# Sparse attention and a gated FFN on one core: two dense groups of 128 tokens become one of 256, and the instruction order is a new one

## The chip, the cores and the metric

The kernel runs on one core of a Trainium2 chip. Times are device microseconds from launch to end; the time of a kernel is the median of its runs. A profiled execution gives one trace, whose times count from the span's start. PE is the matrix engine (TensorE), DVE the vector engine, ACT the scalar engine, POOL is GpSimd, and SP (SyncE) issues DMAs, as POOL does. PE writes into PSUM, eight banks of 2 KB per partition, from which ACT and DVE read.

## The reference

Block-sparse attention over 4 batches, 8 heads, 768 positions and 64 dims, followed by a gated feed-forward over all 3072 tokens:

```python
scores = scale * np.matmul(q, k.transpose(0, 1, 3, 2))
mask = np.abs(blk_i - blk_j) <= 1            # blocks of 32: own and neighbours
mask = mask | (blk_i == 0) | (blk_j == 0) | (blk_i == 23) | (blk_j == 23)
for qb in range(24):
    for kb in sampled_blocks[qb]:            # three sampled blocks per query block
        mask[qb*32:(qb+1)*32, kb*32:(kb+1)*32] = True
attn = softmax(np.where(mask, scores, -1e9))
attn_out = np.matmul(attn, v)                # -> x: 3072 tokens x 512
gate = 1.0 / (1.0 + np.exp(-(x @ w_gate)))   # 512 x 1536
out = (gate * (x @ w_val)) @ w_out           # 1536 x 512
```

## The kernel before, in words

**Attention.** Each batch has 24 query blocks. Blocks 0 and 23 see all keys and are done "edge-wise" (`dsc`, `dmx`, `dex`, `dsl`, `dtp`, `dte`, `dpv`, `dxe`). The other 22 are done as eleven pairs, or steps: (4,5), (6,7) ... (18,19), (2,3), (20,21), (1,22). A name like `sc0_18` is an operation, batch 0, and the first block of its pair. A step is, in turn: `kw` copies the neighbour keys and `kg` (POOL, line 712) the three sampled key blocks into a key tile KG; `sc` makes scores and mask on PE (lines 784 and 773) in two PSUM banks; `mx` (DVE, line 796) takes the row maximum; two `ex` (ACT, line 806, two exponentials each) make P and free one bank each; `rz` inverts the sums; two `sl` scale P, on ACT (line 828), DVE (830, two instructions) or POOL (824, one instruction of 512 columns); `tp` transposes P on PE (842); `te` copies that to PTS on DVE or ACT (848); `pv` multiplies with V on PE (860); `xe` copies the result into XT, the input of the dense stage. V is stored to a scratch in DRAM (`scr`), from which windows of neighbours (`w`) and sampled blocks (`vg`) are read into the tiles V1 and V2, A to D; the two edge blocks of V are copied into these by `vfl`, on POOL two copies (line 641).

**Dense stage.** Tokens go through in groups of 128-token tiles; `groups` in TUNE lists the (batch, tile) pairs of each. For each of 12 chunks of 128 hidden units, `pg` and `pu` (line 1029, four matmuls each: one slot) multiply the group's columns of XT with `w_gate` and `w_val`, into one PSUM bank each; `th` (ACT, line 1038) takes tanh of the first and frees its bank, `h` (DVE, line 1043) multiplies it with the second and frees that. Then `py` (line 1060) makes 128 rows of the output, `ys` evicts them and `st` stores them. A group needs its tiles' attention: tile (0, 1) is blocks 4 to 7 of batch 0, tile (0, 2) blocks 8 to 11. All groups use banks 5, 6 and 7, but the first `two` groups use only 5 and 6:

```python
def pg_of(g):
    return bk(5, 6) if g < TUNE["two"] else pgb if g < len(GROUPS) - 2 else pgb + bk(4, 3, 2, 1, 0)
```

**Order.** The program order on every engine is written out in the string ORDER, one item per operation: `sl0_40:A` says that this operation runs on ACT; digits behind the engine choose among buffers or banks; `+14` behind a PE operation puts 14 fillers ahead of it, matmuls of a zero tile WZ into bank 7 whose result nobody reads (line 1083). Every engine does its items in that order and waits for what an item needs. POOL's list holds its DMAs as well: the loads of q, k and v, of the weights (`wg0`, `wv0` ... `wo2`, in thirds) and some windows.

Of the kernel before, what the change touches and what calls it, by code (L numbers as in the profile page):

```python
# [55 lines left out]
wg1:G sc0_4:P3+14 mx0_4:D6 kw0_10:G0 sc0_6:P1+1 kg0_10:G dsl0_00:D ex0_40:A0 mx0_6:D0 dtp0_00:P00+5 ex0_41:A w0_4:G0
vg0_5:S dte0_00:D regPOOL0_1:G ex0_60:A2 dtp0_01:P0+4 vg0_7:S rz0_4:D sl0_41:D ex0_61:A sc0_8:P0 sc0_10:P3 kw0_14:D2
sl0_40:A rz0_6:D mx0_8:D7 vg0_4:S kw0_12:A1 tp0_4:P11+3 dte0_01:A mx0_10:D1 kg0_12:G vg0_6:S sl0_60:A dpv0_0:P0+4
w0_8:G0 sl0_61:D ex0_80:A1 te0_4:D wv1:G vg0_8:S ex0_81:A sc0_12:P2+2 tp0_6:P10 kw0_18:G1 ex0_100:A0 vg0_11:S
kg0_14:G te0_6:D ex0_101:A mx0_12:D0 pv0_4:P1+3 wg2:G vg0_9:S kg0_18:G rz0_8:D rz0_10:D ex0_120:A2 xe0_4:D dxe0_0:D  # L60
vg0_10:S sl0_100:A sl0_80:G pv0_6:P0+8 sl0_101:A sc0_14:P0 wv2:G xe0_6:D kw0_2:A2 sl0_81:D w0_12:G0 pg0_0:P00+2
pu0_0:P1 th0_0:A0 tp0_10:P12 h0_0:D kw0_16:D0 pg0_1:P10 regSP0_1:S mx0_14:D1 pu0_1:P0 kg0_16:G th0_1:A2 tp0_8:P00
ex0_121:A pg0_2:P10 h0_1:D wo0:G te0_10:D pu0_2:P0+1 th0_2:A2 ex0_140:A0 pg0_3:P10 vg0_13:S h0_2:D regPOOL0_2:G
rz0_12:D sl0_120:D pu0_3:P0 th0_3:A0 sl0_121:A pg0_4:P10+1 h0_3:D te0_8:D pu0_4:P0 th0_4:A2 vg0_12:S ex0_141:A
sc0_16:P2 h0_4:D pg0_5:P10 mx0_16:D5 pv0_8:P1 kw0_20:A0 pu0_5:P0 w0_16:S0 tp0_12:P00 th0_5:A1 kg0_20:G ex0_160:A1
h0_5:D vg0_15:S rz0_14:D sl0_141:D pg0_6:P00+1 pu0_6:P1 te0_12:D th0_6:A0 w0_2:G0 xe0_8:A sc0_18:P0 h0_6:D pg0_7:P00
mx0_18:D4 pu0_7:P1 ex0_161:A pv0_10:P0 vg0_14:S wo1:G th0_7:A1 ex0_180:A2 h0_7:D pg0_8:P00+2 rz0_16:D xe0_10:D
kg0_2:G th0_8:A2 vg0_19:S sl0_160:D pu0_8:P0+3 pg0_9:P10 kw0_1:G1 sl0_161:D sc0_2:P2 h0_8:D th0_9:A1 ex0_181:A wo2:G
pu0_9:P0 mx0_2:D7 vg0_18:S pg0_10:P10 tp0_16:P02 kg0_1:G th0_10:A0 pu0_10:P1 h0_9:D ex0_20:A1 pg0_11:P00 h0_10:D
sl0_140:G vg0_16:S pu0_11:P1 th0_11:A1 ex0_21:A sc0_20:P0+1 h0_11:D vfl0A:G pg1_0:P10 mx0_20:D3 pu1_0:P0 th1_0:A0  # L70
pg1_1:P20 pu1_1:P1 th1_1:A2 tp0_14:P11 te0_16:A h1_0:D h1_1:D pg1_2:P00 rz0_18:D sl0_181:D pu1_2:P1 ldv10:G0
vg0_17:S pg1_3:P20 th1_2:A2 rz0_2:D pv0_12:P0 h1_2:D th1_3:A0 sl0_20:G pu1_3:P2 xe0_12:A pg1_4:P10 h1_3:D te0_14:D
regSP0_2:S pu1_4:P2 w0_1:G0 th1_4:A0 ex0_200:A0 pg1_5:P10 h1_4:D sl0_180:D pu1_5:P0 pg1_6:P20 sl0_21:D th1_5:A2
pv0_14:P0 th1_6:A0 h1_5:D ldk10:G1 pu1_6:P2 vg0_3:S xe0_14:A pg1_7:P10 h1_6:D pu1_7:P0 ldq10:G2 pg1_8:P20 th1_7:A2
sc0_1:P2 h1_7:D th1_8:A0 vfl0B:G ex0_201:A pu1_8:P1 vg0_21:S mx0_1:D2 pg1_9:P00 tp0_18:P10 th1_9:A2 pu1_9:P2
pg1_10:P00 h1_8:D rz0_20:D tp0_2:P01 h1_9:D vg0_20:S th1_10:A0 sl0_201:D ex0_10:A2 pu1_10:P2 pg1_11:P10 h1_10:D
pu1_11:P2 th1_11:A0 sl0_200:A dsc0_23:P02 h1_11:D ex0_11:A py1_0:P2 dmx0_231:D1 vg0_2:S rz0_1:D dmx0_230:D4
dex0_231:A0 dex0_230:A1 dsl0_231:D py0_0:P1 sl0_11:D te0_2:A ys1_0:D0 dsl0_230:D te0_18:A vsh1:D3 dtp0_230:P00
ys0_0:A1 rrk1:G0 scr1:S dtp0_231:P1 dte0_230:D dte0_231:D pv0_16:P0 tp0_20:P12 xe0_16:D te0_20:D rrq1:G1 trk100:P0
evk100:D trk102:P1 st0_0:S pv0_18:P0 evk102:D st1_0:S dpv0_23:P1 regPOOL1_2:G vg0_1:S xe0_18:D pg2_0:P10 dxe0_23:D  # L80
pu2_0:P0 vg0_22:S th2_0:A0 trq102:P0 pg2_1:P10 evq102:D trk101:P1 th2_1:A2 h2_0:D trk103:P0 gv1:S evk101:A pu2_1:P2
ldv20:G0 evk103:D pg2_2:P00 h2_1:D kw1_1:A0 pu2_2:P1 kfl11:G trq101:P1 kfl10:G th2_2:A1 trq100:P0 evq101:D kg1_1:G
pg2_3:P20 evq100:A h2_2:D trq103:P1 pu2_3:P1 kw1_2:A1 evq103:D th2_3:A1 sc1_1:P1 kg1_2:G pv0_2:P1 mx1_1:D3 pg2_4:P00
ldk20:G1 pu2_4:P2 th2_4:A2 xe0_2:D ex1_10:A0 kw1_20:G0 pg2_5:P00 sl0_10:D pv0_20:P0 ex1_11:A h2_3:D sc1_2:P0 vfl1C:S
h2_4:D tp0_1:P12 mx1_2:D4 kw1_4:G1 th2_5:A0 pu2_5:P1 kg1_20:G te0_1:A w1_2:S0 pg2_6:P00 h2_5:D pu2_6:P2 th2_6:A2
rz1_1:D regPOOL1_0:G sl1_11:D pg2_7:P10 regSP1_2:S h2_6:D pu2_7:P0 th2_7:A0 xe0_20:D pg2_8:P20 ex1_20:A1 pu2_8:P1
sl1_10:D pv0_1:P1 h2_7:D th2_8:A2 kg1_4:G ex1_21:A pg2_9:P20 h2_8:D w1_1:S0 sc1_20:P2 vfl1D:G th2_9:A2 pu2_9:P0
mx1_20:D1 xe0_1:A vg1_3:S pg2_10:P10 pu2_10:P2 th2_10:A0 h2_9:D tp1_1:P00 ex1_200:A2 h2_10:D pg2_11:P10 vg1_21:S
kw1_6:D0 pu2_11:P0 rz1_2:D th2_11:A0 sl1_21:G pg3_0:P20 h2_11:D sc1_4:P0 th3_0:A1 vg1_22:S sl1_20:G ex1_201:A
py2_0:P0 mx1_4:D6 kg1_6:G rrk2:D2 vg1_1:S ex1_40:A0 ex1_41:A vsh2:D1 pu3_0:P2 vg1_2:S tp1_2:P11 kw1_8:A1 te1_1:D  # L90
# [1025 lines left out]
```

## Time and profile before

| | us |
|---|---|
| three runs | 339.26, 339.18, 337.01 |
| median | 339.18 |
| profiled execution | 338.43 |
| its span, first to last instruction | 336.5 |
| busy: PE, DVE, ACT, POOL | 318.1, 230.8, 232.4, 128.1 |
| PE busy with fillers (102) | 28.5 |

An instruction row of the profile's order of time gives start, duration, engine, line, operation, output and inputs, shapes, a count where several were merged, and in brackets the idle time of the engine ahead of it with what ended it. A row of the table of stretches gives the stretch, its length, the busy time of PE, of PE's weight loads (PEld), DVE, ACT and POOL with their instruction counts, then the granted TensorE clock (1.00 is full), the DMA share and the GB/s. A row on a group gives count, busy time, mean ns of one, idle time ahead; a row on a tile or line gives shortest, median and longest ns, and first and last start. Matmuls are pipelined: the next can start before the one ahead has ended.

### The profile page before, as it was taken

The numbers are of one execution on the slowest core, as the hardware profiler recorded it, in microseconds if no ns is written. First come the engines' busy times: TensorE is split into PE (matmuls) and PEld (weight loads), VectorE is DVE, ScalarE is ACT, GpSimd is POOL, SyncE is SP. The second block draws the span as 40 slices with busy tenths as digits, with TensorE's granted clock in tenths as the row PEclk, the third lists the DMA queues.
The fourth block names the chain that finished last, engine by engine and source line by source line (L and its number), as shares of the span: only waits on it lengthen the run. The fifth ranks groups of instructions, "written<-read, shape, count | busy, mean of one in ns | idle before, by whom it ended". The sixth has DMA issues, their size and how long they took to land.

```text
span 336.5 us, 11685 instructions
## 1 busy us (share of the span) xinstructions
PE 318.1 (95%) x4230; PEld 194.5 (58%) x4230; DVE 230.8 (69%) x493; ACT 232.4 (69%) x663; POOL 128.1 (38%) x376
## 2 busy tenths in 40 slices
PE   8999887899999789999998999999999999999995
PEld 3545565748776667796555655555645555554442
DVE  3677787777888896697878687698986855423330
ACT  1759785782789887866886788898999764523320
POOL 6575774614777433353184414522522100000000
PEclk9999997999999999999999999999999999999999
DMA  7999999986976655476984344241242352011002
GB/s 115 206 233 216 179 260 209 181 155 186 150 168 100 162 171 157 133 116 129 216 162 125 92 123 134 69 132 33 51 130 70 108 150 52 7 57 64 0 31 94
DMA packets 42873, 43.14 MB, mean 128 GB/s; under 512 B 6560, under 2 KB 39200, under 8 KB 42720
## 3 DMA queue, kind: packets, MB, share of 16 engines
q0 software_dynamic: 14736, 15.93, 29.5%
q1 hardware_dynamic: 28080, 26.47, 27.0%
q8 instruction: 33, 0.54, 0.7%
q14 instruction: 24, 0.20, 0.2%
HBM read 47.10 MB, written 9.44 MB: 168 GB/s over the span
## 4 chain that ended last, share of the span: by engine, by line
PE 70%; DMA 8%; DVE 8%; ACT 7%; issue 3%; POOL 2%; SPq 1%; POOLq 0%; DVEq 0%; ACTq 0%
PE pall L1029 32%; PE pall L1060 17%; PE pall L860 6%; PE pall L842 4%; DMA stg<-in_v_dram 4%; ACT P L806 4%; PE pall L784 3%; PE pall L551 2%; PE pall L970 2%; DVE HT L1043 2%; DMA V2C<-scr 2%; DMA scr<-XL 2%; ACT TH L1038 2%; PE pall L950 1%; DVE NM L796 1%
## 5 line engine op out<-in xcount | busy, mean ns | idle before, releaser
L1038 ACT ACTIVATE TH<-pall 128x512 f32<-128x512 f32 (+2 forms) x108 | 49.1, 459 | 54.7 <-PE pall L1029 46.7
L806 ACT ACTIVATE P<-pall,NM 128x256 f16<-128x256 f32 x176 | 81.3, 477 | 6.5 <-DVE NM L796 5.7
L1043 DVE SCALAR_TENSOR_TENSOR HT<-TH,pall 128x512 f16<-128x512 f32 (+2 forms) x108 | 53.6, 506 | 33.3 <-PE pall L1029 27.3
L1060 PE MATMUL pall<-wo,HT 128*128 128x512 f16 x288 | 65.5, 379 | 0.2 <-DVE HT L1043 0.2
L796 DVE TENSOR_REDUCE NM<-pall 128x4 f32<-128x1024 f32 x44 | 53.6, 1220 | 14.5 <-PE pall L773 9.7
L712 POOL COPY KG<-KT 128x64 f32 x264 | 53.0, 251 | 24.8 <-PE pall L773 18.4
L1029 PE MATMUL pall<-XT,wv 128*128 128x256 f16 (+2 forms) x336 | 56.1, 290 | 4.4 <-DVE HT L1043 3.7
L1029 PE MATMUL pall<-XT,wg 128*128 128x256 f16 (+2 forms) x336 | 56.0, 290 | 3.7 <-DVE HT L1043 1.9
L1029 PEld LDWEIGHTS <-wg 128*128 128x128 f16 x432 | 37.8, 98 | 28.9 <-issue 8.2
L1029 PEld LDWEIGHTS <-wv 128*128 128x128 f16 x432 | 37.8, 99 | 26.7 <-issue 7.3
L1060 PEld LDWEIGHTS <-HT 128*128 128x128 f16 x288 | 26.9, 98 | 32.0 <-issue 1.2
L806 ACT ACTIVATION_READ_ACCUMULATOR P<-pall,NM 128x1 f32 x176 | 36.8, 209 | 0.0
L824 POOL TENSOR_TENSOR P<-P,ZZ 128x512 f16<-128x512 f16 x19 | 19.6, 1039 | 31.8 <-DVE ZZ L815 12.9
L1083 PE MATMUL pall<-WZ 128*128 128x512 f16 x102 | 28.5, 414 | 1.2 <-DVE WZ L371 1.2
L828 ACT ACTIVATE P<-P,ZZ 128x256 f16<-128x256 f16 x54 | 24.4, 514 | 4.7 <-DVE ZZ L815 4.7
L842 PE MATMUL pall<-ident,P 128*128 128x128 f16 x352 | 26.9, 219 | 0.1
L842 PEld LDWEIGHTS <-P 128*128 128x128 f16 x352 | 22.1, 98 | 5.1 <-issue 1.5
L1029 PE MATMUL pall<-XL,wg 128*128 128x512 f16 x96 | 24.0, 379 | 0.0
L1029 PE MATMUL pall<-XL,wv 128*128 128x512 f16 x96 | 24.0, 379 | 0.0
L848 ACT COPY PTS<-pall 128x1024 f16<-128x1024 f16 x21 | 21.2, 1016 | 3.7 <-PE pall L842 3.6
L830 DVE TENSOR_SCALAR P<-P,ZZ 128x256 f16<-128x256 f16 x84 | 23.2, 330 | 0.6
L784 PE MATMUL pall<-KG,QT 64*32 64x256 f16 x704 | 18.8, 277 | 1.2 <-ACT P L806 0.8
(106 smaller groups left out, 448.1 us busy)
## 6 DMA issues: line engine op xcount, KB each, us to landing
out_dram<-YS SPq DMA_DIRECT2D x24, 256.0 KB, 2.0
stg<-in_q_dram POOLq DMA_DIRECT2D x4, 768.0 KB, 9.7
stg<-in_v_dram POOLq DMA_DIRECT2D x4, 768.0 KB, 8.7
V2C<-scr SPq DMA_DIRECT2D x96, 32.0 KB, 2.7
V2D<-scr SPq DMA_DIRECT2D x78, 32.0 KB, 2.6
stg<-in_k_dram POOLq DMA_DIRECT2D x3, 768.0 KB, 8.6
scr<-stg SPq DMA_DIRECT2D x12, 192.0 KB
wg<-in_moe_w_gate_dram POOLq DMA_DIRECT2D x3, 512.0 KB, 8.0
```

The lines of the kernel that those rows point to most:

```text
L712: pin(nc.gpsimd.tensor_copy(t[:, :, u, KO[r] + (2 + n) * BLK : KO[r] + (3 + n) * BLK].bitcast(f32), KT[r].bitcast(f32)[:, :, bass.ds(regs[ ...
L784: pin(nc.tensor.matmul(t[32 * p : 32 * p + 32, hh, u * 256 + c0 : u * 256 + c1], QT[r][kp, p, i * BLK : (i + 1) * BLK], src, start=(merged ...
L796: pin(nc.vector.tensor_reduce(NM[o.slots[hz][1]][:, 0:4].rearrange("p (h u) -> p h u", h=2), t, axis=AX.X, op=ALU.max, negate=True))
L806: pin(nc.scalar.activation(pb[:, hh, u, :], t[:, hh, u * 256 : u * 256 + 256], AF.Exp, bias=NM[z][:, 2 * hh + u : 2 * hh + u + 1], scale=1 ...
L828: pin(nc.scalar.activation(pb[:, u, :], pb[:, u, :], AF.Copy, scale=z[:, 2 * hh + u : 2 * hh + u + 1]))
L830: pin(nc.vector.tensor_scalar(pb[:, u, :], in0=pb[:, u, :], scalar1=z[:, 2 * hh + u : 2 * hh + u + 1], scalar2=None, op0=ALU.mult))
L842: pin(nc.tensor.transpose(t[:, m * 128 : m * 128 + 128], pb[:, hh, u, c * 128 : c * 128 + 128], ident))
L1029: pin(nc.tensor.matmul(t, wt[:, c, f_ * 128 : f_ * 128 + 128], XT[g][:, c, :], start=(c == 0), stop=(c == 3)))
L1038: pin(nc.scalar.activation(TH[o.slots[ht][1]][:, 0:n], banks[pl.handles[hg][1]][:, 0:n], AF.Tanh, bias=0.0, scale=0.5))
L1043: pin(nc.vector.scalar_tensor_tensor(HT[:, f_, hoff : hoff + n], in0=TH[pl.handles[ht][1]][:, 0:n], scalar=1.0, in1=banks[pl.handles[hv][1 ...
L1060: pin(nc.tensor.matmul(t, HT[:, f_, hoff + tt * 128 : hoff + tt * 128 + 128], wo[:, f_, :], start=(f_ == 0), stop=(f_ == NF - 1)))
L1083: pin(nc.tensor.matmul(banks[7], WZ[:, 0:128], WZ, start=True, stop=True))
```

## The change

```diff
-TUNE = {'groups': [[(0, 1)], [(0, 2)], [(0, 3), (0, 4)], [(0, 0), (0, 5)], [(1, 0), (1, 5)],
+TUNE = {'groups': [[(0, 1), (0, 2)], [(0, 3), (0, 4)], [(0, 0), (0, 5)], [(1, 0), (1, 5)],
             [(1, 1), (1, 2), (1, 3), (1, 4)], [(2, 0), (2, 5), (2, 1), (2, 2)],
             [(2, 3), (2, 4), (3, 0), (3, 5)], [(3, 1), (3, 2), (3, 3), (3, 4)]],
...
- 'two': 1,
+ 'two': 0,
...
- 'merge': 'mmmm'}
+ 'merge': 'mmmm',
+ 'kdma': 0}
...
-wz:D cdma:S ldk00:G3 gv0:S memset:G ldk01:G ldq00:G1 mask:D ldv00:G2 wg0:G wv0:G idx:D trk000:P2+23 trk001:P3
+wz:D memset:G cdma:S ldk00:G0 gv0:S ldk01:G ldq00:G1 ldv00:G3 mask:D wg0:G wv0:G gc0:A trk000:P1+23 trk001:P2
...
```

Tiles (0, 1) and (0, 2) form one group of 256 columns; groups after it have numbers lower by one, and the first group uses three banks as the others do. `kdma` is read nowhere. The table ORDER is replaced as a whole: 1398 items for 1446, since 24 `pg`/`pu`, 12 `th` and 12 `h` are gone; 124 fillers for 102, all of them now ahead of the first dense slot. Lines of the new kernel are lower by two. The search that made the table, and the operations' lengths that it went by, are not part of the program.

On ACT, at the first attention step of batch 0, before (DP is the P of edge block 0, in two halves; P_96 and P_98 belong to the steps (4,5) and (6,7), QT is the transposed q):

```order
L728 COPY KG_93<-KT_74 128x8x96
L575 ACTIVATE QT_76<-pall 128x768 x3
L933 ACTIVATE DP_118,ZZ_108<-pall,NM_100 128x768
L933 ACTIVATE DP_119,ZZ_110<-pall,NM_102 128x768
L806 ACTIVATE P_96,ZZ_113<-pall,NM_105 128x256 x4
L806 ACTIVATE P_98,ZZ_107<-pall,NM_99 128x256 x4
```

The same place in the new order (P_96 and P_97 are the steps (4,5) and (6,7)):

```order
L573 ACTIVATE QT_76<-pall 128x768 x3
L931 ACTIVATE DP_119,ZZ_114<-pall,NM_106 128x768
L726 COPY KG_92<-KT_74 128x8x96
L804 ACTIVATE P_96,ZZ_111<-pall,NM_103 128x256 x4
L931 ACTIVATE DP_118,ZZ_110<-pall,NM_102 128x768
L804 ACTIVATE P_97,ZZ_114<-pall,NM_106 128x256 x4
```

The second half of the edge block has moved behind the exponentials of the first step; the scores of the second step take a bank that this half frees.

On ACT, where the dense stage begins, before (TH is the output of `th`):

```order
L828 ACTIVATE P_96<-P_96,ZZ_108 128x256 x4
L728 COPY KG_93<-KT_74 128x8x96
L1038 ACTIVATE TH_121<-pall 128x128
L1038 ACTIVATE TH_123<-pall 128x128
L806 ACTIVATE P_98,ZZ_107<-pall,NM_99 128x256 x2
L1038 ACTIVATE TH_123<-pall 128x128
L806 ACTIVATE P_96,ZZ_108<-pall,NM_100 128x256 x2
```

And in the new order (the four exponentials ahead of the first TH belong to the step (16,17)):

```order
L885 CAST XT_132<-pall 64x2x4x32 x2
L826 ACTIVATE P_96<-P_96,ZZ_107 128x256 x2
L726 COPY KG_93<-KT_74 128x8x96
L804 ACTIVATE P_97,ZZ_108<-pall,NM_100 128x256 x4
L1036 ACTIVATE TH_122<-pall 128x256
L804 ACTIVATE P_98,ZZ_109<-pall,NM_101 128x256 x2
L1036 ACTIVATE TH_123<-pall 128x256
```

The first `th` stands behind the exponentials of step (16,17) instead of between those of (12,13), and works on 256 columns.

On POOL, late in batch 0, before (P is scaled in `TENSOR_TENSOR` rows, GV holds the edge blocks of V):

```order
L641 COPY V1A<-GV 32x1024
L641 COPY V2A<-GV 32x1024
L417 DMA stg_78<-in_v_dram 96x8x512
L824 TENSOR_TENSOR P_97<-P_97,ZZ_114 128x512
L676 DMA V1D<-scr_126 96x512 x2
L417 DMA stg_79<-in_k_dram 96x8x512
L417 DMA stg_80<-in_q_dram 96x8x512
L641 COPY V1B<-GV 32x1024
L641 COPY V2B<-GV 32x1024
```

And in the new order:

```order
L822 TENSOR_TENSOR P_96<-P_96,ZZ_111 128x512
L674 DMA V1C<-scr_126 96x2x512 x2
L639 COPY V1B<-GV 32x1024
L639 COPY V2B<-GV 32x1024
L822 TENSOR_TENSOR P_97<-P_97,ZZ_114 128x512 x2
L822 TENSOR_TENSOR P_98<-P_98,ZZ_113 128x512
L451 TENSOR_LOAD kidx x2
```

Four scalings of P stand here where before has one, and the loads of the next batch have moved ahead. Over the whole program POOL has 33 of them for 19, ACT 21 `sl` for 27 and DVE 34 for 42; `te` is on ACT 11 times for 21 and on DVE 33 times for 23; `vfl` is on POOL 9 times for 5.

More of the change, by code (lines that the diff above doesn't have):

```diff
@@ L56 @@
[L56 to L90, printed above, removed]
@@ L171 @@
+pu7_2:P7 th7_2:A1 pu7_9:P3 pg7_7:P51 h7_9:D pu7_7:P1 th7_7:A0 pg7_10:P01 h7_7:D pu7_10:P2 pg7_4:P10 pu7_4:P4
+th7_4:A2 pg7_11:P61 h7_4:D pg7_3:P50 th7_10:A2 h7_10:D pu7_3:P4 th7_3:A0 h7_2:D pu7_11:P2 h7_3:D pg7_6:P11 th7_11:A0
+h7_11:D pu7_6:P4 th7_6:A2 pg7_8:P50 h7_6:D pu7_8:P6 th7_8:A2 pg7_5:P21 pu7_5:P1 th7_5:A1 pg7_1:P31 h7_5:D h7_8:D
+pu7_1:P4 th7_1:A0 h7_1:D py7_0:P5 py7_1:P3 ys7_0:D1 st7_0:S py7_3:P6 ys7_1:A0 st7_1:S py7_2:P4 ys7_3:D1 st7_3:S
+ys7_2:A0 st7_2:S
 """
```

193 lines of the change are left out of this document (110 added, 83 removed).

## The prediction

> **What bounds the kernel now.** I read the page's head first, then the table of stretches, then the order of time around the places where TensorE (PE) waits.
>
> ```profile
> span 336.5 us, 11685 instructions
> PE 318.1 (95%) x4230; PEld 194.5 (58%) x4230; DVE 230.8 (69%) x493; ACT 232.4 (69%) x663; POOL 128.1 (38%) x376
> ```
>
> The PE row shows 95%, and no other engine comes above 69%. But part of it is dummy work: 102 matmuls on the zero tile WZ, all ahead of or inside batch 0. So the end is set by PE's useful work, which both kernels share, plus fillers, plus waits. The stretches show where waits lie; the first number pair after the core's stretch is PE's busy time.
>
> ```profile
> 1.20:38.40 37.20, 35.40 (x477) 17.57 (x478) 23.92 (x52) 23.33 (x61) 26.01 (x75) 1.00 1.07 196
> 46.90:68.10 21.20, 17.47 (x328) 13.78 (x328) 15.93 (x41) 14.46 (x58) 13.47 (x27) 0.92 1.11 209
> 80.10:97.50 17.40, 17.30 (x294) 14.64 (x291) 13.67 (x33) 13.54 (x42) 9.95 (x35) 1.00 0.91 173
> 97.50:128.00 30.50, 27.46 (x442) 19.94 (x439) 25.62 (x56) 27.21 (x83) 16.29 (x46) 1.00 0.55 130
> 128.00:248.00 120.00, 118.14 (x1748) 74.10 (x1752) 93.22 (x190) 97.04 (x276) 49.67 (x153) 1.00 0.49 121
> 248.00:336.50 88.50, 84.13 (x704) 41.98 (x681) 40.67 (x82) 43.33 (x110) 4.58 (x24) 1.00 0.21 66
> ```
>
> PE is idle for 3.7 us of 46.9 to 68.1 (first and second dense group), for 3.0 of 97.5 to 128, where ACT is busy 27.2 of 30.5, and for only 1.9 of the 120 us after that. The last row's 4.4 us are mostly the last eviction and store. So the head of the program, up to about 68 us, is a chain of attention steps with dense work between; from there on PE is nearly full. The granted clock was 0.92 in the second stretch, 1.00 in the others.
>
> **The dense rows.** The first group of before (128 columns) and the third (256), each after the step that it follows:
>
> ```profile
> 46.90 0.41 PE L784 MATMUL pall<-KG,QT 64*32 64x256 f16 x16 [0.18 <-ACT P L806]
> 47.12 0.28 PE L773 MATMUL pall<-mrow,ones 64*32 64x192 bf16 x8
> 47.33 0.40 PE L1029 MATMUL pall<-XT,wg 128*128 128x128 f16 x4
> 47.56 0.39 PE L1029 MATMUL pall<-XT,wv 128*128 128x128 f16 x4
> ```
>
> ```profile
> 91.60 0.60 PE L1029 MATMUL pall<-XT,wg 128*128 128x256 f16 x4
> 92.03 0.60 PE L1029 MATMUL pall<-XT,wv 128*128 128x256 f16 x4
> ```
>
> Start to start, four matmuls of 128 columns take 0.23 us and four of 256 take 0.43; an attention step on PE (scores with their mask, 46.90 to 47.33) takes 0.43, and I take 0.45 for any of them. So the merge is worth little on PE itself: 48 slots x 0.225 = 10.8 us become 24 x 0.43 = 10.3, **-0.5 us**. The Trainium skill, "TensorE: Matmul & The Clock Gate", section "Back-to-back issue gap", puts a sustained pair of weight load and matmul at about 81 ns for 128 columns; by that, 192 matmuls would take 15.6 us and the merge would save 5.2. These rows have 57 ns, and the sum goes by them.
>
> On the evicting engines it saves twelve tanh on ACT and twelve products on DVE. That lies beside PE work and is no term by itself.
>
> **Term 1, up to the scores of blocks 18 and 19** (46.90 in before, where 14 of the 48 dense slots are done; in the changed order the step just ahead of the first dense row). Here the new order has 124 fillers instead of 102, all ahead of the first dense row, and none of its 24 slots.
>
> ```profile
> 1.21 7.80 PE L1083 MATMUL pall<-WZ 128*128 128x512 f16 x23 [1.21 <-DVE WZ L371]
> ...
> 18.55 3.20 PE L1083 MATMUL pall<-WZ 128*128 128x512 f16 x14
> ...
> 20.37 0.90 ACT L933 ACTIVATE DP<-pall,NM 128x768 f16<-128x768 f32 x1 [2.65 <-DVE NM L927]
> ...
> 21.67 0.41 PE L784 MATMUL pall<-KG,QT 64*32 64x256 f16 x16
> ...
> 22.25 1.22 DVE L796 TENSOR_REDUCE NM<-pall 128x4 f32<-128x1024 f32 x1 [0.24 <-PE pall L773]
> 22.42 0.41 PE L784 MATMUL pall<-KG,QT 64*32 64x256 f16 x16
> ```
>
> A lower bound by counting: 1.2 + 7.7 for the first 23 fillers + 101 x 0.215 (the row of 14: 3.20 less a last matmul's 0.4, over 13) + 28 attention steps x 0.45 = 43.3 us. The chain says later. The first scores start as before, near 21.4, since the same exponential (20.37) frees their banks. The second ones started at 22.42; now the other exponential of the edge block stands behind four exponentials of the first pair (the first ACT rows of the change), so they wait for 21.4 + 0.5 scores + 1.2 row maximum + 4 x 0.48 + 0.9 = 25.9, 3.5 us later. It doesn't stay lost: before needs 24.5 us for the six scores from there to 46.90, with 14 dense slots and their evictions between, and these are gone. The next scores but one wait for the banks of the second: 25.9 + 0.5 + 0.3 for a scaling that DVE does first + 1.2 + 4 x 0.48 = 29.8, say 30.1 with the hand-overs; the one between has other banks. From there four more follow at one per scores 0.45 + maximum 1.2 + two exponentials 0.95, which free the bank that the next one needs, + 1.3 estimated for the scaling or copy that stands ahead of them on ACT: 3.95 us each. 30.1 + 15.8 = **45.9**, against 46.90. Bounds: 43.3 by the count; 47.7 if PE also loses the 1.8 us that it idled in 1.20:38.40. I take the chain, since nearly each link has a row. The key load moves behind 0.9 us of constants on POOL, which the first 23 fillers (until 9.0 us) hide; the second value-weight chunk is issued some 5 us earlier, among the window loads, and is covered because the window products, which wait for these windows, come some 4 us later than before. Were that cover gone, the wait would be that of one chunk beside the windows, 1 to 2 us, inside the bounds.
>
> **Term 2, from there to the scores of block 23.** In before this is 46.90 to 68.10:
>
> ```profile
> 68.09 0.84 PE L916 MATMUL pall<-KT,QT 64*32 64x384 f16 x16
> ```
>
> Before's work in it: 34 slots x 0.225 + 11 attention steps x 0.45 + 6 fillers x 0.215 = 13.9 of 21.2 us, so 7.3 were lost, 1.4 of them to the clock (8% of 17.5). The change has 24 slots x 0.43 + 10 x 0.45 = 14.9 us and no filler. What is lost with it? Nothing at best. The nearest row is the 256-column group at 80.1 to 97.5, on the same three banks between attention steps: 24 x 0.435 + 8 x 0.45 + 6 transposes of keys and queries x 0.34 (the row below is two of them) = 16.1 of 17.4, so 1.3 lost. At worst, the same 7.3. I take 2.7: that row, and one more hold of the kind shown next, since the copies of V into the windows still run in this stage. 45.9 + 14.9 + 2.7 = 63.5, **-4.6 us**; bounds -7.3 and 0, and -2.6 to +1.8 more from term 1.
>
> ```profile
> 83.96 0.68 PE pall L551 x16
> ```
>
> **Term 3, the remaining 268 us.** The same PE work in nearly the same order. What changes is who does the elementwise steps. Counting names in the two tables: evictions of transposed probabilities on ACT 21 to 11 (DVE 23 to 33), scalings of probabilities on ACT 27 to 21, DVE 42 to 34, POOL 19 to 33, and copies of V edges on POOL 5 to 9.
>
> ```profile
> L848 DVE COPY PTS<-pall x23: 659/683/693, 30.0 to 278.6; 128x1024 f16<-128x1024 f16 x23
> L848 ACT COPY PTS<-pall x21: 990/1012/1067, 58.5 to 295.8; 128x1024 f16<-128x1024 f16 x21
> ```
>
> ```profile
> L828 ACT ACTIVATE P<-P,ZZ x54: 491/510/551, 27.1 to 294.7; 128x256 f16<-128x256 f16 x54
> ```
>
> ```profile
> L824 POOL TENSOR_TENSOR P<-P,ZZ x19: 1028/1038/1070, 35.3 to 242.0; 128x512 f16<-128x512 f16 x19
> ```
>
> ACT loses 10 x 1.01 us of evictions and six scalings of two 0.51 us instructions, 16 us; DVE gains 10 x 0.68 and loses eight pairs of 0.28, about +2; POOL gains 14 x 1.04 + 4 x 2.2 (two copies as in the row at 51.67 below) = 23 us of long instructions. Other moves between ACT and DVE about cancel. Where ACT is full (97.5 to 128) PE waits 3.0 us; I take those as gone. Against it stands what POOL's long instructions do to DVE:
>
> ```profile
> 53.44 0.38 PE L1029 MATMUL pall<-XT,wv 128*128 128x128 f16 x4 [2.41 <-DVE HT L1043]
> ...
> 179.39 0.81 PE L1029 MATMUL pall<-XT,wg 128*128 128x512 f16 x3 [1.42 <-DVE HT L1043]
> ```
>
> ```profile
> 50.00 3.06 DVE L830 TENSOR_SCALAR P<-P,ZZ 128x256 f16<-128x256 f16 x4
> ...
> 174.53 2.03 DVE L728 COPY KG<-KT 128x768 f16<-128x768 f16 x1
> ```
>
> ```profile
> 50.58 1.03 POOL L824 TENSOR_TENSOR P<-P,ZZ 128x512 f16<-128x512 f16 x1
> 51.67 1.12 POOL L641 COPY V1A<-GV 32x1024 f32<-32x1024 f32 x1
> ```
>
> ```profile
> L830 DVE TENSOR_SCALAR P<-P,ZZ x84: 269/281/1691, 25.8 to 274.6; 128x256 f16<-128x256 f16 x84
> ```
>
> Two of PE's longest waits, 2.41 and 1.42 us, stand right behind a DVE instruction that took up to 1.69 us where 0.28 is usual, or 2.03 in a copy, while POOL was at products and edge copies, or, the second time, at key copies, whose number stays. Of the first kind before has 29 (19 products, 10 edge copies) and the change 22 more: 2.41 x 22/29 = 1.8, or 2.9 with both waits. A part is in term 2, so I add 1.6. Term 3 is -3.0 + 1.6 = **-1.4 us**; bounds -4.9 (all idle from 97.5 to 248 gone) and +2.9.
>
> **The sum.** The profiled execution took 338.43 us, 1.9 more than its span, and lies 0.75 under the median of the three runs shown. 338.4 - 4.6 - 1.4 = **332.4**; the merge's 0.5 is inside term 2.
>
> **Rivals.**
> *Given back.* A 256-column slot holds its bank through the matmuls, tanh or product, and with 24 slots on three banks any exponential ahead of a tanh on ACT stops PE, just as in before. Then term 2 loses 7.3 again, block 23 comes near 68, and with term 3 the time is 337; for it speaks that DVE and ACT are already busy 13.7 and 13.5 of the 17.4 us beside such a group; against it, that PE idled only 0.1 there. 0.25.
>
> *Slower: POOL holds DVE.* Each added long POOL instruction can stop a DVE copy or scaling for some 0.95 us (the four at 50.00 took 3.06 where 4 x 0.28 = 1.1 is usual, in two holds), and DVE's next product keeps a dense bank closed, in the groups of batches 0 to 2. All 22 on PE's path cost 21 us. Without the 1.6 of term 3 the sum is 330.8, so from 12 such holds on (11 us) it is slower by over 1%; with 14 it is 344. For it: the two waits above. Against: of the 29 in before few did harm, and DVE has fewer such scalings to be stopped. 0.18. The Trainium skill, "SBUF — State Buffer", section "Who interferes with whom", has a rule for this: a VectorE copy or scaling in a two-port mode and a GpSimd instruction exclude each other for the whole instruction. By that rule every overlap costs the full length, which is what the 1.69 us shows.
>
> *More than forecast.*
>
> ```profile
> L1029 PEld LDWEIGHTS <-wg 128*128 128x128 f16 x432 | 37.8, 98 | 28.9 <-issue 8.2
> ```
>
> If the 48 slots of 128 columns are paced by weight loads of 98 ns that don't overlap, they cost 18.8 us, the merge saves 8 us more, and the time is 324. The 0.23 us above, with four such loads inside, speak against it. 0.07.
>
> **How the numbers follow.** Forecast 0.50, at 332.4 with 329 to 335 as its own range. A measurement of this kernel tells about 1% (3.4 us) from no change. Faster by over 1%: 0.50 + 0.07 less a little of the forecast's upper end = 0.55; within 1%: 0.27; slower: 0.18. The range goes from 326 (most of the way to the fast rival) to 343 (just short of the slow one's 344); the terms' bounds alone allow 324 to 343.
>
> **What would show it.** Second scores near 26 us and the first 256-column dense row near 46; block 23's scores (the second L916 group by line of before) at 61 to 65. PE idle in the stage after it under 2 us per 30. DVE's scalings with a maximum under 2 us and few above 1. Wrong if the first dense row comes after 48, if block 23 comes after 67, or if the DVE holds sum to more than some 9 us.

## The result, and the profile after

The changed kernel takes **347.30 us** (median of four runs, 344.29 to 348.78), the kernel before beside it 339.22 (337.01 to 340.93): **1.029 times as long**, 95% interval 1.023 to 1.035. The prediction was 332.4 us, with 0.18 for slower.

The head of the profile's page after the change; the profiled execution took 348.78 us, 1.8 more than its span:

```profile
span 347.0 us, 11477 instructions
PE 321.3 (93%) x4156; PEld 194.9 (56%) x4156; DVE 232.1 (67%) x469; ACT 218.8 (63%) x630; POOL 149.1 (43%) x399
```

ACT fell by 13.6 us and POOL rose by 21 (16 and 23 were counted ahead), and PE is busy 3.2 us more, with 22 more fillers. But the span grew by 10.5 us: PE waits longer. The table of stretches of the changed kernel shows where. Its rows give the stretch, its length, busy time of PE, PEld, DVE, ACT and POOL with counts, the granted clock, the DMA share and GB/s.

```profile
38.00:44.00 6.00, 0.28 (x4) 0.12 (x4) 0.64 (x3) 0.93 (x3) 4.10 (x10) 0.82 0.82 189
44.00:49.00 5.00, 5.00 (x54) 2.87 (x54) 1.50 (x2) 0.86 (x4) 3.82 (x9) 0.53 1.10 172
54.60:72.00 17.40, 16.17 (x272) 13.06 (x274) 13.99 (x34) 12.96 (x49) 8.97 (x15) 1.00 0.71 125
101.00:132.00 31.00, 25.97 (x400) 18.20 (x398) 27.54 (x54) 25.33 (x80) 16.10 (x38) 1.00 0.55 127
132.00:252.00 120.00, 116.87 (x1707) 74.51 (x1705) 96.89 (x199) 87.92 (x254) 55.87 (x160) 0.99 0.46 115
```

There are two places. In the head, six microseconds in which PE does 0.28 us of work and DVE and ACT less than 1 each, and behind them five at about half the clock. Later, 101 to 132, PE is idle for 5.0 us (before, 97.5 to 128, 3.0), and from 132 to 252 for 3.1 (before 1.9).

**The head.** The changed kernel in order of time on PE: the second scores, the first value product, and block 23's scores.

```profile
25.63 0.41 PE L782 MATMUL pall<-KG,QT 64*32 64x256 f16 x16 [0.31 <-ACT DP L931]
...
38.03 0.19 PE L858 MATMUL pall<-PTS,V1C 128*128 128x64 f16 x1 [1.04 <-DVE PTS L846]
43.91 0.21 PE L858 MATMUL pall<-PTS,V2C 128*128 128x64 f16 x1 [5.69 <-DMA V2C<-scr]
...
71.96 0.84 PE L914 MATMUL pall<-KT,QT 64*32 64x384 f16 x16
```

The first value product begins at 38.03 and its second matmul waits 5.69 us for a gather of V. What the gather waited for stands on SP's queue, in order of time, first of the changed kernel:

```profile
24.36 0.33 SPq L674 DMA_DIRECT2D V1C<-scr  x1
24.90 3.80 SPq L743 DMA_DIRECT2D V2C<-scr  x6
28.88 7.08 SPq L743 DMA_DIRECT2D V2D<-scr  x3
```

The row of SP's waits in the changed kernel (total, times, longest) that lies in the last of these:

```profile
SPq L743 <- DMA V1C<-scr: 5.8, 1, 5.8
```

And SP's queue in the kernel before:

```profile
25.19 5.91 SPq L745 DMA_DIRECT2D V2C<-scr  x12
31.28 9.38 SPq L745 DMA_DIRECT2D V2D<-scr  x12
```

Before, SP issues twelve gathers in 5.9 us. After, SP issues the window of blocks 4 to 7 first (V1C, 384 KB) and then stops for 5.8 us inside the third group of gathers, until that window has landed; the chain that ended last gives its landing as 10.76 us after the issue. Block 4's gathers, the fourth group, come behind that, and the last of them lands 6.63 us after its own issue, at 43.82. The rows of the new order on SP show why a gather waits for a window into another tile (the last is the eighth gather behind it):

```
6 L674 DMA V1C<-scr_126 96x4x512 [waits DMAHW4_49]
8 L743 DMA V2C<-scr_126 32x512
...
18 L743 DMA V2C<-scr_126 32x512 [waits DMAHW3_49]
20 L743 DMA V2D<-scr_126 32x512
22 L743 DMA V2D<-scr_126 32x512 [waits DMAHW5_49]
```

The program lets each of SP's DMAs raise one of eight semaphores, 0 to 7 in turn, and the eighth DMA behind one reuses its semaphore, so it waits for that one's landing. A gather of 32 KB has landed by then or nearly so (in the kernel before, SP's longest wait for one up to 60 us is 0.8 us); a window that takes 10.76 us has not.

**The rest.** From block 23's scores to the span's end it is 275.0 us, 268.4 before: 6.6 us more. PE's two longest waits there are one of 1.90 us for YS (from 106.5) and one of 2.80 for XT (from 189.7), both DVE's. DVE in order of time just ahead of them:

```profile
104.70 3.03 DVE L828 TENSOR_SCALAR P<-P,ZZ 128x256 f16<-128x256 f16 x2
...
184.70 2.17 DVE L828 TENSOR_SCALAR P<-P,ZZ 128x256 f16<-128x256 f16 x2
...
187.59 2.19 DVE L828 TENSOR_SCALAR P<-P,ZZ 128x256 f16<-128x256 f16 x2
```

What POOL does meanwhile:

```profile
103.80 1.11 POOL L710 COPY KG<-KT 128x64 f32 x6
104.86 1.89 POOL L533 COPY stg<-stg 96x2048 f32<-96x2048 f32 x1
106.70 1.12 POOL L710 COPY KG<-KT 128x64 f32 x6
...
187.62 1.89 POOL L533 COPY stg<-stg 96x2048 f32<-96x2048 f32 x1
```

The row of DVE's scalings in the whole program (shortest, median, longest ns):

```profile
L828 DVE TENSOR_SCALAR P<-P,ZZ x68: 256/281/2833, 29.9 to 289.7; 128x256 f16<-128x256 f16 x68
```

Two scalings that usually take 0.56 us together took 3.03, 2.17 and 2.19 while POOL was at work. Over the whole program DVE's scalings took 9.5 us beyond 0.28 each, 4.4 in the kernel before. The wait of 2.80 us has an echo: from 192.1 to 195.4 the granted clock is 0.50.

### The profile page after: what moved, and what is told of

Same layout as the page of the kernel before. It is cut to its first block, busy times and chain, and to the rows that moved or that the text cites. A ratio compares the mean times of both kernels' runs of the same rounds, so it can differ in the third digit from the quotient of the medians.

```text
span 347.0 us, 11477 instructions
## 1 busy us (share of the span) xinstructions
PE 321.3 (93%) x4156; PEld 194.9 (56%) x4156; DVE 232.1 (67%) x469; ACT 218.8 (63%) x630; POOL 149.1 (43%) x399
## 4 chain that ended last, share of the span: by engine, by line
PE 72%; DMA 11%; DVE 9%; ACT 4%; issue 2%; POOL 1%; SPq 0%; DVEq 0%; ACTq 0%; POOLq 0%
PE pall L1027 32%; PE pall L1058 17%; PE pall L858 6%; PE pall L840 4%; DMA stg<-in_v_dram 4%; PE pall L782 3%; DMA V1C<-scr 3%; DVE NM L794 2%; PE pall L549 2%; DVE HT L1041 2%; PE pall L968 2%; ACT P L804 2%; DMA V2C<-scr 2%; DMA scr<-XL 2%; PE pall L948 1%
## 5 line engine op out<-in xcount | busy, mean ns | idle before, releaser
L1041 DVE SCALAR_TENSOR_TENSOR HT<-TH,pall 128x256 f16<-128x256 f32 (+1 forms) x96 | 51.7, 547 | 38.3 <-PE pall L1027 29.9
L1036 ACT ACTIVATE TH<-pall 128x256 f32<-128x256 f32 (+1 forms) x96 | 46.6, 492 | 39.8 <-PE pall L1027 33.0
L822 POOL TENSOR_TENSOR P<-P,ZZ 128x512 f16<-128x512 f16 x33 | 34.1, 1043 | 60.0 <-DVE ZZ L813 22.4
L1027 PE MATMUL pall<-XT,wg 128*128 128x256 f16 (+1 forms) x288 | 53.6, 308 | 3.8 <-DVE YS L1065 1.9
L1027 PE MATMUL pall<-XT,wv 128*128 128x256 f16 (+1 forms) x288 | 53.7, 309 | 0.3 <-ACT TH L1036 0.3
L1027 PEld LDWEIGHTS <-wg 128*128 128x128 f16 x384 | 35.2, 98 | 27.6 <-issue 7.5
L1081 PE MATMUL pall<-WZ 128*128 128x512 f16 x124 | 32.7, 405 | 1.2 <-DVE WZ L369 1.2
L726 POOL COPY KG<-KT 128x384 f32<-128x384 f32 (+1 forms) x23 | 11.5, 503 | 35.7 <-PE pall L771 19.7
L846 DVE COPY PTS<-pall 128x1024 f16<-128x1024 f16 x33 | 22.4, 681 | 4.9 <-PE pall L840 4.7
L1067 ACT ACTIVATE YS<-pall 128x512 f32<-128x512 f32 x17 | 10.0, 597 | 16.9 <-PE pall L1058 16.8
```

Source lines behind the costliest of these rows:

```text
L822: pin(nc.gpsimd.tensor_tensor(pb, pb, z[:, 2 * hh : 2 * hh + 2].unsqueeze(2).broadcast_to([128, 2, 256]), op=ALU.mult))
L846: pin(copy(o)(PTS[pl.handles[hTS][1]].rearrange("p m n -> p (m n)"), banks[pl.handles[hT][1]].bitcast(f16)))
L1027: pin(nc.tensor.matmul(t, wt[:, c, f_ * 128 : f_ * 128 + 128], XT[g][:, c, :], start=(c == 0), stop=(c == 3)))
L1036: pin(nc.scalar.activation(TH[o.slots[ht][1]][:, 0:n], banks[pl.handles[hg][1]][:, 0:n], AF.Tanh, bias=0.0, scale=0.5))
L1041: pin(nc.vector.scalar_tensor_tensor(HT[:, f_, hoff : hoff + n], in0=TH[pl.handles[ht][1]][:, 0:n], scalar=1.0, in1=banks[pl.handles[hv][1 ...
L1081: pin(nc.tensor.matmul(banks[7], WZ[:, 0:128], WZ, start=True, stop=True))
```

## Experiments

Each run is told by its ratio to the kernel before on the same chip; places in time are from its profiled execution, which can lie 1 to 2 us from the median. All edits are to items of the table ORDER; where groups are merged or split, `groups` goes with them.

### The window and the weight chunk

The window back on POOL:

```diff
-... wv1:G ex0_41:A w0_4:S0 vg0_7:S ...
+... wv1:G ex0_41:A w0_4:G0 vg0_7:S ...
```

> The changed kernel with one edit: the window of blocks 4 to 7 (V1C<-scr, 384 KB) is issued by POOL, where the kernel before has it, instead of by SP ahead of the gathers. In the changed kernel SP issues it at 24.36 us, it lands after 10.76 us, and SP's second gather for V2D waits 5.8 us for that landing. Theory Q (the queue): this wait of SP is what makes the first value product's second matmul wait 5.69 us for V2C. Then SP's longest wait between 24 and 45 us falls under 2 us, the last V2C gather lands some 5 us earlier (near 38), the scores of blocks 18 and 19 come near 49 instead of 54.6, and the time falls by 4 to 6 us, to 341 to 343. Theory B (the bytes): the second chunk of the value weights, issued at 22.32 us ahead of the windows, takes the transfers' rate; the gathers then land late whoever issues the window, the scores of 18 and 19 stay after 53, and the time falls by at most 1.5 us, to 346 to 347.

The second chunk of the value weights behind the windows:

```diff
-... dmx0_00:D3 wv1:G ex0_41:A w0_4:S0 ...
+... dmx0_00:D3 ex0_41:A w0_4:S0 ...
...
-... w0_8:G0 ... w0_12:G0 rz0_4:D ...
+... w0_8:G0 ... w0_12:G0 wv1:G rz0_4:D ...
```

> The changed kernel with one edit: POOL issues the second chunk of the value weights (wv1, 512 KB) behind the windows of blocks 4 to 15 instead of ahead of them. Theory B (the bytes): the window on SP, which lands after 10.76 us in the changed kernel, then lands in 5 to 6 us, as it does on POOL in the kernel before (4.5); SP's wait of 5.8 us shrinks to under 1.5, the scores of 18 and 19 come near 50, and the time falls by 4 to 5 us, to 342 to 343. Theory Q (the queue): the other two windows still fill the same 5 us, the window lands after 8 us or more, SP still waits 3 us or more, and the time falls by at most 2 us, to 345 or more.

Both edits:

> The changed kernel with both edits: the window of blocks 4 to 7 on POOL, and wv1 behind the windows. If theories Q and B name two ways to the same wait of 5.7 us, the result is that of the better of the two single edits, 341 to 343. If each takes its own part, the gains add, but not past the place where the first value product waits for no transfer: at most 7.7 us up to the scores of 18 and 19 (54.6 against 46.9 in the kernel before), so 339.5 to 341. In both cases the rest of the program, from block 23's scores on, keeps its 275 us (268.4 before), so that the time stays at or above that of the kernel before.

Measured: window on POOL 342.69 us, 1.017 of the kernel before (1.009 to 1.024); chunk late 342.79, 1.017 (1.009 to 1.025); both 341.57, 1.013 (1.005 to 1.021). The three can't be told apart. The scores of blocks 18 and 19 come at 47.7, 48.0 and 47.8 us, block 23's at 64.3, 64.5 and 64.4. SP with the window on POOL:

```profile
24.51 2.99 SPq L743 DMA_DIRECT2D V2C<-scr  x6
...
30.85 4.00 SPq L743 DMA_DIRECT2D V2C<-scr  x6
```

and SP's wait for the window in the run with the chunk late, where the window stays on SP and lands after 5.42 us:

```profile
SPq L743 <- DMA V1C<-scr: 1.4, 1, 1.4
```

So each theory was right on its own edit and wrong on the other's: Q said that the late chunk would leave 3 us of SP's wait, B that the window on POOL would leave the gathers late, but either edit takes the 5.69 us away (0.3 us of a wait for V2C is left with the window on POOL; with the chunk late PE waits 1.1 us for the gathers of V2D instead). It needs both: a window slow to land, because the chunk shares the transfers with it (with the chunk behind it, the window lands after 5.42 us), and SP waiting for it. 6.9 us go up to the scores of 18 and 19, more than the wait itself. These stretches of the run with the window on POOL show the rest, beside the first two rows of the table above:

```profile
38.00:44.00 6.00, 5.52 (x115) 3.48 (x114) 4.50 (x12) 3.22 (x13) 3.96 (x10) 1.00 0.94 211
44.00:49.00 5.00, 4.65 (x82) 2.78 (x67) 3.94 (x6) 4.36 (x14) 4.90 (x16) 1.00 1.03 164
```

Without the wait the clock stays at 1.00, where it was 0.53.

The other way round, in the kernel before:

```diff
-wg1:G sc0_4:P3+14 ... ex0_41:A w0_4:G0
-vg0_5:S ... te0_4:D wv1:G vg0_8:S
+wg1:G wv1:G sc0_4:P3+14 ... ex0_41:A
+w0_4:S0 vg0_5:S ... te0_4:D vg0_8:S
```

> The other way round: the kernel before, unmerged, with the two moves of the changed kernel's order that the runs so far have singled out: the window of blocks 4 to 7 issued by SP ahead of the gathers, and wv1 by POOL right behind wg1, ahead of the windows. If these two together are the cause, the window takes 8 to 11 us to land instead of 4.5, SP waits for it at its eighth gather by 3 us or more, the first value product (33.3 us in the kernel before) waits for V2C to 38 or later, and the time rises by 3 to 7 us, to 341 to 345. If the changed kernel's wait needs its own order of blocks (its first value product needs the fourth group of gathers, here it is the third), the time stays within 1.5 us of the kernel before.

Measured: 343.96 us, 1.018 (1.011 to 1.025). PE in order of time:

```profile
34.36 0.20 PE L860 MATMUL pall<-PTS,V1C 128*128 128x64 f16 x1 [1.37 <-DVE ZZ L815]
39.74 0.21 PE L860 MATMUL pall<-PTS,V2C 128*128 128x64 f16 x1 [5.17 <-DMA V2C<-scr]
```

and SP's wait:

```profile
SPq L745 <- DMA V1C<-scr: 4.3, 1, 4.3
```

The same wait at the same matmul, 5.17 us, and block 23 at 75.0 instead of 68.1; the window lands after 9.39 us. The cause is made by the two items together, without the merge, and unmade by either, with it.

### The held scalings

Changed kernel with the window on POOL, and three pairs of scalings on ACT:

```diff
-sl1_201:D ... sl2_20:D ... sl2_201:D
+sl1_201:A ... sl2_20:A ... sl2_201:A
```

> The changed kernel with the window of blocks 4 to 7 on POOL (as in the run before this), and three pairs of scalings moved from DVE to ACT: those that DVE shows at 96.90, 176.77 and 179.65 us in that run, with 2.83, 2.16 and 2.19 us for two instructions that usually take 0.56 together, each while POOL copies. Theory H (POOL holds DVE there, and PE waits for what stands behind on DVE): DVE is 7.2 us freer at those places, PE's waits of 1.71 us for YS at 100.38 and of 2.78 us for XT at 184.53 fall below 0.6 each, and the time falls by 3 to 4.5 us against the run with the window alone, so to 338 to 340 beside a kernel before of 337.2. Theory W (the waits come from the order, whoever scales): ACT takes 1.03 us for a pair and has rows of its own behind them; PE's two waits stay above 1.2 us each, and the time stays within 1 us of 342.7.

The same, but with POOL's copies moved instead:

```diff
-rrk2:G2 ... rrq3:G0
+rrk2:D2 ... rrq3:D0
```

> The changed kernel with the window of blocks 4 to 7 on POOL, and two of POOL's copies stg<-stg (1.89 us each at 97.03 and 179.68 us in that run, beside the long scalings) done by DVE instead, which shows 1.14 us or less for the same kind elsewhere in its own order; the scalings stay on DVE. Theory H: the scalings beside them take at most 1 us instead of 2.83 and 2.19, so DVE gains some 2.8 us in two holds (those beside its POOL copies of KG stay) and pays 2.3 us for the copies; PE's waits for YS and XT fall by 1 us or more each, and the time falls by 1 to 3 us. Theory W: the two waits stay, DVE only has 2.3 us more to do, and the time stays or rises by up to 2 us.

The changed kernel with the three scalings alone, its window and chunk untouched:

> The changed kernel, its window and its weight chunk as they are, with only the three pairs of scalings moved from DVE to ACT. If the window (before block 23's scores) and the held scalings (behind them) are two causes that add, this run keeps the head (the scores of 18 and 19 near 54.6, block 23's near 72) and takes only the tail's part: 4 to 5 us off, 342 to 344 beside a kernel before of 337 to 339, about as much above the kernel before as the window alone cost. If the tail's waits are an echo of the late head, they come back at another place and the time stays above 346.

Measured: scalings on ACT 336.45 us, 0.989 (0.984 to 0.994); copies on DVE 337.63, 0.997 (0.993 to 1.000); scalings alone, window untouched, 344.68, 1.019 (1.010 to 1.029). Rows of PE's waits from 64 us on, with the window on POOL alone:

```profile
PE pall L858 <- DVE XT L994: 2.8, 1, 2.8
PE pall L1027 <- DVE YS L1065: 1.7, 1, 1.7
```

with the scalings on ACT:

```profile
PE pall L858 <- DMA V2B<-scr: 1.7, 1, 1.7
...
PE pall L858 <- DVE XT L994: 0.6, 1, 0.6
```

DVE with the copies moved, at the place where the scalings had taken 2.83 in the run with the window alone:

```profile
96.79 0.48 DVE L828 TENSOR_SCALAR P<-P,ZZ 128x256 f16<-128x256 f16 x2
97.64 0.69 DVE L1065 TENSOR_SCALAR YS<-pall 128x512 f32<-128x512 f32 x1 [0.36 <-PE pall L1058]
98.25 1.27 DVE L530 COPY stg<-stg 96x4096 f16<-96x4096 f16 x1
```

Both gains are larger than expected (338 to 340 us with the scalings, 1 to 3 us for the copies), that of the scalings alone is a little smaller (342 to 344). Theory H holds: with POOL's copy gone the same two scalings, still on DVE, take 0.48, and the wait for YS is gone; the one for XT is 1.08 with the copies moved, 0.6 with the scalings moved, where a gather (V2B, 1.7 us) is late next. From block 23's scores to the last matmul it is 271.2 us with the window alone, 267.8 with the scalings on ACT, 267.1 with the copies on DVE. The last run leaves the head nearly as it was (54.7 and 73.0 us, the second 1.0 later) and takes 5.3 us from the tail: in the traces the two losses are separate. Spans add up: 7.6 us less with the window alone, 4.3 with the scalings alone, 11.8 with both. The medians don't: the single edits take 1.2% and 1.0%, both together 4.0%. Part of the difference to the spans is that the changed kernel's profiled execution was the slowest of its four and that of the window run the fastest; why the pair gains more than its parts in the medians isn't known.

### The merge by itself

The kernel before, groups merged: the first group's 48 operations are out, and the second tile's rows, now of 256 columns, stand where they stood. Ten fillers that stood ahead of the removed rows went with them (92 for 102), so the merge isn't quite alone.

```diff
-... pg0_0:P00 pu0_0:P1 th0_0:A0 ... h0_0:D pg0_1:P10 ... pg1_0:P10 ... pu1_0:P0 th1_0:A0
+... pg0_0:P10 ... pu0_0:P0 th0_0:A0
```

> The kernel before with the merge alone: its order of work is kept, the first group's 48 operations are taken out, and the second tile's rows (now 256 columns) stand where the second group's stood. Theory O (the new order loses the time, the merge as such costs nothing): the time is that of the kernel before within 2 us, 337 to 341. Theory M (the merge itself costs, since PE has no dense rows of the first tile to run between the attention of the second): PE's fillers do not grow by themselves, so PE waits for the exponentials and scalings between the scores of blocks 14 and 20, up to the 10.6 us that the first group's rows take there, and the scores of 20 and 21 stay where they were while 11 us of dense rows are added behind them: 346 to 350.

Measured: 342.08 us, 1.015 (1.007 to 1.023): more than O's 2 us, less than M's. Without the first tile's rows PE waits between the attention steps, as M says (its three longest rows from 33 to 71 us):

```profile
PE pall L784 <- ACT P L806: 3.8, 2, 2.3
PE pall L784 <- DVE P L830: 2.4, 1, 2.4
PE pall L784 <- POOL KG L712: 1.5, 1, 1.5
```

and from 45.2 to 70.3 us the granted clock is 0.76; how much of that is due to the ten fillers isn't shown. But block 23 comes at 70.3, only 2.2 us later than before, as the scores no longer stand behind dense rows (those of 20 and 21 come at 53.3 instead of 56.4). In the trace the last matmul ends at 333.6 us, 0.8 later than before; this execution was the fastest of its four.

Then the mended head of the changed kernel (window on POOL, chunk late) up to block 23's scores, and from there the order of the kernel before with the merge:

> The merge with the better half of each order: up to block 23's scores the changed kernel's order with the window on POOL and wv1 behind the windows (these scores at 64.4 us there), from there on the order of the kernel before with the merge alone (from those scores at 70.3 us to the last matmul at 333.6 us, 263.3 us). If the loss of the changed kernel sits in two separate places (the window in the head, waits on DVE in the tail), the halves add: last matmul near 327.7 us against 332.8 in the kernel before, and the time 331 to 334 beside 337 to 339 of the kernel before. If instead what the head wins is only taken from the tail (work left over that the tail has to do), the last matmul stays near 333 and the time near that of the kernel before, 336 to 339.

Measured: **333.49 us, 0.983 (0.980 to 0.987)**, faster than the kernel before and than the changed one. Block 23 at 64.8, last matmul at 328.6. The page's head:

```profile
span 332.7 us, 11490 instructions
PE 317.4 (95%) x4156; PEld 193.0 (58%) x4156; DVE 226.6 (68%) x484; ACT 226.9 (68%) x645; POOL 130.2 (39%) x377
```

and the row of DVE's scalings:

```profile
L828 DVE TENSOR_SCALAR P<-P,ZZ x84: 271/280/1064, 29.9 to 270.6; 128x256 f16<-128x256 f16 x84
```

With the tail of the kernel before, POOL is busy 19 us less than in the changed kernel, and no scaling takes more than 1.06 us. The halves add (last matmul expected near 327.7).

In this kernel, the merge alone undone (at each place the row of the first tile, then that of the second):

```diff
-pg0_0:P10 ... pu0_0:P2 th0_0:A1 ... h0_0:D
+pg0_0:P00 pu0_0:P1 th0_0:A0 ... pg1_0:P20 h0_0:D pu1_0:P0 th1_0:A1 h1_0:D
```

> The order that is faster than both (the mended head of the changed kernel, the tail of the kernel before), with the merge alone undone: at each place of a row of 256 columns of the first group stand the same row for the first tile and then for the second, 128 columns each, with a tanh and a product for each. What the merge is worth by itself: PE's rows differ by 0.5 us in all as predicted (96 matmuls of 256 columns against 192 of 128), and ACT and DVE get 24 short instructions more each. If the prediction's sum for the merge holds, the time is within 1.5 us of the merged one, 332.5 to 335. If short rows cost PE more than their start-to-start time says, or if the three banks are too few for them, so that PE waits for their evictions, the last matmul comes 3 to 8 us later.

Measured: 339.54 us, 1.005 (1.001 to 1.008), 2.2% above the merged one by these ratios (1.5% by the spans of the traces); last matmul at 333.6, 5.0 us later. The stage of the dense group, merged, as a stretch and as the row of PE's wait for DVE's products in it:

```profile
48.70:64.80 16.10, 15.53 (x262) 12.83 (x250) 13.85 (x34) 12.12 (x45) 9.27 (x17) 1.00 1.09 192
```

```profile
PE pall L1027 <- DVE HT L1041: 0.4, 1, 0.4
```

The same two, split, and then four of the split rows in order of time:

```profile
47.80:69.30 21.50, 17.59 (x344) 15.15 (x336) 15.36 (x46) 14.33 (x59) 9.91 (x21) 1.00 1.07 189
```

```profile
PE pall L1027 <- DVE HT L1041: 3.7, 7, 1.2
```

```profile
54.55 0.38 PE L1027 MATMUL pall<-XT,wg 128*128 128x128 f16 x4 [0.46 <-DVE HT L1041]
54.77 0.39 PE L1027 MATMUL pall<-XT,wv 128*128 128x128 f16 x4
54.99 0.39 PE L1027 MATMUL pall<-XT,wg 128*128 128x128 f16 x4
55.30 0.38 PE L1027 MATMUL pall<-XT,wv 128*128 128x128 f16 x4
```

The second expectation comes true, in its second form: rows start 0.22 us after one another, as costed, except where they wait for a bank. Seven waits for DVE's products sum to 3.7 us; and the fourth row of most chunks starts 0.31 us or more after the third, behind a tanh, which sums to about 1 us more. So PE waits for evictions, and its rows are no longer than costed. The split rows use the three banks in an order of their own, and no other was tried: the 2.2% are shown for this order of work and these banks.

### The fillers

The window on POOL, the chunk late, and 23 fillers behind the first value product taken out:

```diff
-pv0_4:P0+3 ... tp0_8:P10+5 ... pv0_6:P1+4 ... pv0_8:P0+2 ... pv0_10:P1+3 ... sc0_18:P0+6
+pv0_4:P0 ... tp0_8:P10 ... pv0_6:P1 ... pv0_8:P0 ... pv0_10:P1 ... sc0_18:P0
```

> The changed kernel with the window on POOL and wv1 behind the windows, and without the 23 fillers (0.41 us each, 9.4 us) that its order has behind the first value product. Theory C (they stand in waits that are there anyway): PE's waits grow by what the fillers gave up, the scores of 18 and 19 stay within 1 us of 47.8 and the time within 1.5 us of 341.6. Theory P (once the order is behind its lengths, fillers push the rest back): the scores of 18 and 19 come 2 to 4 us sooner, and the time falls by as much. If the granted clock falls for want of fillers, the rows in the next 30 us are some per cent longer, which would take up to 2 us back.

Measured: 341.55 us, 1.008 (1.005 to 1.012), against 1.013 (1.005 to 1.021) with them; scores of 18 and 19 at 47.3 instead of 47.8. Theory C: they stand in waits that are there anyway. The stretch from 38 to 52 us without them, then with them:

```profile
38.00:52.00 14.00, 10.41 (x183) 7.79 (x183) 9.71 (x22) 9.51 (x33) 9.01 (x25) 0.76 1.09 203
```

```profile
38.00:52.00 14.00, 12.47 (x212) 8.30 (x219) 9.94 (x22) 9.50 (x33) 9.01 (x25) 1.00 1.14 209
```

The clock falls to 0.76 without them, and the waits take that up.

## Why the prediction was wrong, point by point

The forecast's span was 330.5 us (332.4 less 1.9), the measured one 347.0. Of these 16.5 us, 8.7 lie in term 1 (54.6 against 45.9), -0.2 in term 2 and 8.0 in term 3 (+6.6 against -1.4). All three marks of being wrong came: the first dense row at 55.8 us, block 23 at 72.0, DVE holds of 9.5. Two slips in the sums (the link of 3.95 us adds up to 3.90, and 24 x 0.43 + 10 x 0.45 to 14.8) would move the forecast by 0.3 us.

- **Dense rows.** Right as to PE: the rows took what was costed. Wrong was the sentence behind it, that twelve tanh and twelve products less are "no term by itself". Where 24 rows of 256 columns stand close together, as in the new order, 48 rows of 128 on the same three banks wait 3.7 us for their products, and undoing the merge costs 5.0 us in the trace. In the order of the kernel before, where the first tile's rows lie between the attention steps, the merge (with ten fillers less) lost 1.5% instead. The rule of the Trainium skill ("TensorE: Matmul & The Clock Gate", "Back-to-back issue gap", 81 ns for a pair) would give 5.2 us, nearly this sum, but the trace doesn't have it where the rule puts it: the split rows keep 0.22 us for four.
- **Term 1.** The chain was right up to the second scores (25.9 predicted, 25.63) and to the start of the window products ("some 4 us later than before": 33.3 to 38.03). **The step that failed** is "the second value-weight chunk is ... covered because the window products ... come some 4 us later", with its price of "1 to 2 us" were the cover gone. The window's own landing was covered; what was not is the gathers that SP held back until then. I hadn't listed that this window moves from POOL to SP, ahead of every gather. The price was 5.69 us of waiting and, with the clock, 6.9 up to the scores of 18 and 19. Without it they come at 47.7, at the upper bound of 43.3 to 47.7, 1.8 us later than the value taken.
- **Term 2.** 17.6 us forecast from these scores to block 23's, 17.4 in the changed kernel and 16.6 with the window on POOL. Given the mended head, block 23 comes at 64.3 to 64.5 us, in the stated 61 to 65. The rival that gives this back didn't occur.
- **Term 3.** Forecast -1.4, measured +6.6, outside the bounds (-4.9 to +2.9). This step failed too. The -3.0 for a relieved ACT didn't come: in the corresponding stretch PE waits 1.9 us for ACT, as before (1.8), and 3.0 for DVE (0.6). The +1.6 for POOL holding DVE was too small, since it scaled two waits by a count of instructions. The three pairs that were moved, with 6.0 of the 9.5 us that DVE was held, cost 3.4 to 5.3 us of the tail.
- **The rivals.** The slower one had the right mechanism and sign, but not its place or its price: not some twelve to fourteen holds of 0.95 us in products and edge copies, but four over 1.5 us, two of them beside POOL's copies stg<-stg. Both kernels have five of these on POOL, but not the same five: the one at 104.86 is on DVE in the kernel before (1.22 us at 99.74), a move that the count of 22 added instructions doesn't see. The mark set for it (holds of more than some 9 us) was just passed. It explains some 3 to 5 us; the window, for which there was no rival, explains 7.6 by the spans and 1.2% (some 4 us) by the medians.
- **What the merge could have given.** With the window and three scalings mended the changed kernel is 1.1% faster than the kernel before, and with the tail of the kernel before 1.7%, 333.49 us against a forecast of 332.4. The sum was thus near for the merge with an order free of the two faults, not for the order that came with it. That it was near is partly luck: it puts the merge at 0.5 us, where undoing it in that kernel costs 5.0, and its term 3 is about a tail that this kernel doesn't have.

What stays open: which part of the tail's remaining 2 to 4 us (265.8 to 267.8 us with holds mended, 263.9 with the order of before) comes from which of its many moves; and what the merge is worth with other banks for the split rows.

## What to carry to other kernels

When an order is replaced as a whole, list for each DMA queue what now stands ahead of what, and which transfer a later issue must wait out; where the program rotates eight semaphores among a queue's DMAs, as here, a large one in front of many small ones holds all from the eighth on until it has landed, even into other tiles. Price an overlap of POOL and DVE by what stands beside what at the place, not by a count. And separate the change from its new order by a run of each before judging either: here the merge lost 1.5% in the old order and gained 2.2% in the new one, once that was mended.

## What the runs showed of the hardware

- **A wait costs more than its length.** With PE idle for 5.69 us the granted clock of the changed kernel was 0.64, 0.50 and 0.72 in the three stretches of 3 us from 41 to 50; in the run with the merge alone it was 0.50 from 44 to 56 us, behind and within a stretch (38 to 53) in which PE was busy 6.5 of 15 us and its longest wait was 2.4. The kernel before shows the same behind its longest wait of PE, 2.41 us (51.0 to 53.4): 0.53 from 55 to 58. The Trainium skill, "TensorE: Matmul & The Clock Gate", Part 1, "The HAM clock gate", has an idle window of about 3.4 us after which the clock is halved. The 0.50 agrees; that PE must be idle that long does not, since waits of 2.4 us were enough here.
- **A DVE scaling can be held over more than one POOL instruction.** The one that began at 104.70 took 2.83 us: it came to an end neither when POOL's copies of KG ended (104.9) nor at the end of its next copy (106.75), but some 0.8 us into the third group. The Trainium skill, "SBUF — State Buffer", "Who interferes with whom", has the lock last for the whole instruction; here DVE didn't get in at the first two boundaries either. The 1.69 us of the prediction was of this kind: it began at 50.00, beside copies of KG, 0.58 us ahead of the product. Not every POOL instruction holds a scaling: with the copies moved, the one at 96.79 began before the last of six KG copies had ended (97.00), and the two took 0.48 (spans on POOL are rough).
- **The landing time of one transfer** of 384 KB went with the place of the 512 KB chunk more than with the issuing engine. With the chunk behind it took 4.5 us (kernel before, on POOL), 5.5 (both edits, on POOL) and 5.42 (chunk late, on SP); with the chunk ahead 8.1 (window on POOL), 9.39 (the kernel before with the two items, on SP) and 10.76 (changed kernel, on SP).
